# Linear attention on TensorE: keys x values by column halves, queries x state by row halves, queries laid out transposed

## Chip, cores and metric

One core of a Trainium2 chip runs the whole program. The metric is the device time of one execution in microseconds (us). The kernel before ran three times: 1289.58, 1290.80 and 1292.42 us, median 1290.8.

## What is computed

Three layers, one after another. Attention has no softmax, so keys and values collapse into one 64 x 64 state per batch and head:

```python
# batch, heads, seq, head_dim = 8, 8, 576, 64
kv  = np.einsum('bhsd,bhse->bhde', k, v)
out = np.einsum('bhsd,bhde->bhse', q, kv)
rms = np.sqrt(np.mean(out * out, axis=-1, keepdims=True) + 1e-06)
x   = out / rms * g_norm              # then tokens x 512: 4608 x 512
h   = x @ w_in                        # 512 x 2048, weights arrive as float64
x   = (h * np.cos(h)) @ w_out         # 2048 x 512
# routed layer: tokens with x @ w_skip > 0 go to the best of 8 experts
# (w_gate), y = gate * (relu(x @ w1[e]) @ w2[e]), added to x
```

## The kernel before, in words

The 4608 tokens are cut into 12 blocks of 384 tokens (`NB`, `TB`), each of three tiles of 128 tokens (`TPB`). A batch has 576 tokens, so two batches (a pair) fill nine tiles, and the fifth tile of a pair straddles both batches.

**The order of the work.** `dense()` (L772) walks through 192 steps, each a block and one of 16 chunks of 128 hidden units. A step issues twelve matmuls of 384 columns (`mm1`, L305), the elementwise chain of h cos(h) on ScalarE and VectorE (L312 to L327), and, three steps late (`LAG`), nine matmuls of 512 columns (`mm2`, L340). Their operands are float32r, each cut into a high part and a rest, hence three products per operand pair. `slot(i)` (L699) says what goes beside a step. Block 0 runs its first ten chunks, then block 1 all 16, then block 0 the other six; from block 2 on the order is plain. After the last block come the experts (L802 on).

**Attention beside it.** `attend(n, s)` (L552) is one of 16 parts of the attention of block n, issued one block ahead: parts 0, 4 and 8 turn a tile of queries (`attn1`: four transposes on TensorE into a PSUM tile `pt`, L198, and a ScalarE copy, L201, then an SP load of the queries two tiles on), parts 2, 6 and 10 multiply it with the state (`attn2`, L212, or L209 and L210 on a straddling tile, into the PSUM tile `po`), square (ScalarE, L214), sum (VectorE, L215) and take a reciprocal root in eleven small VectorE operations (`rsqrt`), parts 3, 7 and 11 scale it (`norm`, L232), parts 5, 9 and 13 transpose the result and cut it into parts (`attn3`, L244 to L247). Parts 1 and 14 of some blocks, or 1 and 5 of block 1, compute keys x values for half of a batch's heads (`do_kv`) and load the keys and values of a later one on SP's queue.

**Keys x values.** Of a batch's 576 tokens, 512 lie as four per partition on 128 partitions and 64 remain (`krem`, `vrem`, two batches stacked on 128 partitions). A head's product is four products of 128 rows (L171) and one of 64 (L172), all into the same 64 partitions of PSUM: the lower half of the array's columns for even heads, the upper for odd. A head is finished before the next begins:

```python
for i in range(NPAIR // 2):
    for o in range(2):
        h = 2 * i + o
        dst = po[o * DH:(o + 1) * DH, i]
        for c in range(CM):
            T.matmul(dst, kt[:, h, c], vt[:, h, c], start=(c == 0), stop=False)
        T.matmul(dst, r[0][rows, half * 4 + h], r[1][rows, half * 4 + h], start=False, stop=True)
```

Two VectorE copies (L175, L176) put the results of two heads on the diagonal of a 128 x 128 block of zeros, `kvbd`, so that one product of 128 rows serves two heads of queries: four products of 128 x 128 x 128 per tile.

**The start** (L487 to L541). SP issues the loads in the order of need: keys and values of batch 0, remainders, the queries of block 0, then weights in turn with further attention operands. The work goes: keys x values of half the heads, three VectorE copies of queries (L194) and their transposes, the other heads, then `attn2` of three tiles into `acc0` to `acc2`, and `rsqrt`, `norm`, `attn3`. `split_w` (L269) decodes a chunk of float64 weights, given as words, by one ScalarE operation, three of VectorE (L287 to L289), a ScalarE copy and one of GpSimd (L292); 32 chunks are decoded beside the first 26 steps.

PSUM's eight banks: two for `ph`, three for `acc`, two for `pt` (transposes of attention and experts), one for `po`.

Of the kernel before, what the change touches and what calls it, by code (L numbers as in the profile page):

```python
# [23 lines left out]
P = 128  # L24
B, H, S, DH = 8, 8, 576, 64
N = B * S
D = H * DH
# [33 lines left out]
def layers(tc, q, k, v, g_norm, w_in, w_out, w_skip, w_gate, w1, w2, out):  # L61
# [4 lines left out]
    # for each expert, in a region of its own, the tokens that are sent to it with their logits  # L66
    rows = nc.dram_tensor("gate_rows", [E + 1, D], F32, kind="Internal").ap()
# [18 lines left out]
    # ------------------------------------------------------------------ attention and dense layer  # L86
# [5 lines left out]
    ps_t = ctx.enter_context(tc.tile_pool(name="ps_t", bufs=2, space=PS))  # L92
# [20 lines left out]
    # a partition holds successive tokens of the first block  # L113
    G.iota(tok[:, 0:TPB], pattern=[[1, TPB]], base=0, channel_multiplier=TPB)
    G.iota(tok[:, TPB:], pattern=[[P, (NB - 1) * TPB]], base=TB, channel_multiplier=1)
# [4 lines left out]
    bp = patt.enter_context(tc.tile_pool(name="attn2", bufs=2, side="right"))  # L120
    kvbd = [ap.tile([P, NPAIR, P], F32, name=f"kvbd{i}") for i in range(2)]
    for t in kvbd:
        G.memset(t, 0.0)

    rem = {}
    qm = {}
    kvt = {}

    def load_rem(pair):
        rem[pair] = tuple(ap.tile([P, H, DH], F32, name=f"{name}rem") for name in "kv")  # L130
        for i in range(2):
            for r, src in zip(rem[pair], (k, v)):
                SP.dma_start(r[i * SR:(i + 1) * SR], src[2 * pair + i, :, SM:S, :].rearrange("h s d -> s h d"))

    def load_q(t):
        """Tile 4 of a pair of batches holds the last 64 rows of the first and the first 64 of the second."""
        if t == 0:
            # the first three, in longer runs
            r = xp.tile([P, H, TPB, DH], F32, name="xl")
            SP.dma_start(r, q[0, :, 0:TB, :].rearrange("h (p j) d -> p h j d", j=TPB))  # L140
            for j in range(TPB):
                qm[j] = r[:, :, j]
            return
        pair, i = divmod(t, 9)
        r = wp.tile([P, H, DH], F32, name="wo14") if t == 5 else bp.tile([P, H, DH], F32, name="q")
        r0 = i * P
        for j, (lo, hi) in enumerate(((0, S), (S, 2 * S))):
            s0, s1 = max(r0, lo), min(r0 + P, hi)
            if s0 < s1:
                SP.dma_start(r[s0 - r0:s1 - r0], q[2 * pair + j, :, s0 - lo:s1 - lo, :].rearrange("h s d -> s h d"))  # L150
        qm[t] = r

    def load_kv(b, half, pool=ap, names=("kmain", "vmain")):
        hs = slice(half * (H // 2), (half + 1) * (H // 2))
        kt = pool.tile([P, H // 2, CM, DH], F32, name=names[0])
        SP.dma_start(kt, k[b, hs, 0:SM, :].rearrange("h (p c) d -> p h c d", c=CM))
        vt = pool.tile([P, H // 2, CM, DH], F32, name=names[1])
        SP.dma_start(vt, v[b, hs, 0:SM, :].rearrange("h (p c) d -> p h c d", c=CM))
        kvt[b, half] = kt, vt

    def do_kv(b, half):
        kt, vt = kvt.pop((b, half))
        r = rem[b // 2]
        rows = slice((b % 2) * SR, (b % 2) * SR + SR)
        po = ps_o.tile([P, NPAIR // 2, DH], F32, name="po")
# [20 lines left out]
    def attn1(t, s=None):  # L186
        pt = ps_t.tile([P, NPAIR, P], F32, name="pt")
        qt = qm.pop(t)
        if t < TPB:
            if t < 2:  # L190
                c = ap.tile([P, H, DH], F32, name=("xn", "tT")[t])
            else:
                c = st.tile([P, H, DH], F32, name="wt", bufs=4)
            V.tensor_copy(c, qt)  # L194
            qt = c
        qt = qt.rearrange("p h d -> p (h d)")
        for hp in range(NPAIR):
            T.transpose(pt[:, hp], qt[:, hp * P:(hp + 1) * P], ident)  # L198
        if s is None:
            s = ap.tile([P, NPAIR, P], F32, name="tT")  # L200
        A.copy(s, pt)  # L201
        qT[t] = s

    def attn2(t, po, xn, ssq):
        i = t % 9
        s = qT.pop(t)
        for hp in range(NPAIR):
            if i == 4:
                T.matmul(po[0:SR, hp], s[:, hp, 0:SR], kvbd[0][:, hp], start=True, stop=True)  # L209
                T.matmul(po[SR:P, hp], s[:, hp, SR:P], kvbd[1][:, hp], start=True, stop=True)  # L210
            else:
                T.matmul(po[:, hp], s[:, hp], kvbd[0 if i < 4 else 1][:, hp], start=True, stop=True)  # L212
        pov = po.rearrange("p n (two e) -> p (n two) e", two=2)
        A.activation(xn, pov, AF.Square)  # L214
        V.tensor_reduce(out=ssq, in_=xn, op=ALU.add, axis=AX.X)  # L215
        normt[t] = xn, pov
# [13 lines left out]
    def norm(t, y):  # L230
        xn, pov = normt.pop(t)
        o = V.tensor_tensor(out=xn, in0=pov, in1=y.unsqueeze(2).to_broadcast([P, H, DH]), op=ALU.mult)  # L232
        xnt[t] = xn
        return o

    def attn3(t):
# [5 lines left out]
        pt = ps_t.tile([P, KD, P], F32, name="pt")  # L242
# [6 lines left out]
    def new_w(which, f):  # L249
        """The two parts of a chunk of the first or the second weights."""  # L250
        if which == "i":
            wi[f] = wp.tile([P, 2, KD, P], F32R, name=f"wi{f}")
            return wi[f][:, 0], wi[f][:, 1]
        wo[f] = wp.tile([P, 2, D], F32R, name=f"wo{f}")
        return wo[f][:, 0], wo[f][:, 1]


    # a chunk's words lie where its two parts will
    def load_w(which, f):
        if f >= NF:  # L260
            return
        if which == "i":
            t = words[which, f] = wp.tile([P, KD, 2 * P], I32, name=f"wi{f}")
            SP.dma_start(t, w_in[:, 2 * f * P:2 * (f + 1) * P].rearrange("(c p) w -> p c w", p=P))
        else:
            t = words[which, f] = wp.tile([P, 2 * D], I32, name=f"wo{f}")
            SP.dma_start(t, w_out[f * P:(f + 1) * P, :])
# [41 lines left out]
    def chain_head(ph):  # L309
        """h cos(h) of h in turns: the nearest whole number off, then cos as a sine."""  # L310
# [38 lines left out]
    def hold(b):  # L349
        """Lays the sums over the first half of a block's chunks aside."""  # L350
        for j in range(TPB):
            t = st.tile([P, D], F32, name=f"tT{j}")
            (V.tensor_copy if j == 1 else A.copy)(t, acc[b][j])
            SP.dma_start(held[j * P:(j + 1) * P, :], t)

    def evac(b):
# [5 lines left out]
        for j in range(TPB):  # L362
# [7 lines left out]
            SP.dma_start(out[0:TB].rearrange("(p j) d -> p j d", j=TPB)[:, j] if b == 0 else out[r0:r0 + P, :], t[:, j])  # L370
# [8 lines left out]

    def score_pe1(b, s, j):  # L380
        pt = ps_t.tile([P, KD, P], F32, name="pt")
# [10 lines left out]
    def route(b, j0, n):  # L392
        """Sends tokens of n tiles of a block to the lists of their experts."""
# [39 lines left out]
    # experts' weights come in pieces of two chunks of rows; an expert's parts take the places of one half of  # L433
    # the dense layer's chunks, in turn: a chunk of the first weights those of two chunks, four tiles each
# [34 lines left out]
    # start  # L469
# [29 lines left out]
    for i in range(2):  # L499
        SP.dma_start(g2[i * DH:(i + 1) * DH], g_norm.unsqueeze(1))  # L500
# [434 lines left out]
```

## Time and profile before

| | us |
|---|---|
| median of three runs (lowest, highest) | 1290.8 (1289.58, 1292.42) |
| profiled execution, span (the time that is given of it) | 1291.6 |
| TensorE matmuls busy | 1242.5 (96%) |
| TensorE weight loads busy (beside matmuls) | 1107.2 (86%) |
| VectorE busy | 870.2 (67%) |
| ScalarE busy | 641.0 (50%) |
| GpSimd busy | 194.2 (15%) |
| DMA, mean over the span | 81 GB/s |

Busy shares are averages over stages with different limits. A matmul's duration runs from its start to its modelled end; neighbours overlap, so what an instruction occupies of TensorE is read from the distance of starts. In rows of the trace, PE is TensorE's matmuls, PEld its weight loads, DVE VectorE, ACT ScalarE, POOL GpSimd; an arrow `<-` behind idle time names what ended it. `128*64` in a TensorE row is the part of the array used, rows by columns, `128x64` the moving operand.

### The profile page before, as it was taken

The numbers are of one execution on the slowest core, as the hardware profiler recorded it, in microseconds if no ns is written. First come the engines' busy times: TensorE is split into PE (matmuls) and PEld (weight loads), VectorE is DVE, ScalarE is ACT, GpSimd is POOL, SyncE is SP. The second block draws the span as 40 slices with busy tenths as digits, with TensorE's granted clock in tenths as the row PEclk, the third lists the DMA queues.
The fourth block names the chain that finished last, engine by engine and source line by source line (L and its number), as shares of the span: only waits on it lengthen the run. The fifth ranks groups of instructions, "written<-read, shape, count | busy, mean of one in ns | idle before, by whom it ended". The sixth has DMA issues, their size and how long they took to land. (4 is left out here: it accounts for less than half of the span.)

```text
span 1291.6 us, 18853 instructions
## 1 busy us (share of the span) xinstructions
PE 1242.5 (96%) x6864; PEld 1107.2 (86%) x6864; DVE 870.2 (67%) x2215; ACT 641.0 (50%) x1215; POOL 194.2 (15%) x187
## 2 busy tenths in 40 slices
PE   5798999999999999999999999999989999999997
PEld 4676898898989889889898989999868889998886
DVE  3988968885949568495774948677694576655421
ACT  2655764455545455555554545555556354444310
POOL 1533202101000000100001000010353312212100
PEclk9789999999999999999999999999999999999999
DMA  9923132203011120210203001010322356444300
GB/s 306 330 90 97 35 122 66 91 9 85 14 32 51 33 75 9 66 34 10 66 9 98 18 9 34 9 33 3 134 81 91 114 171 201 135 158 163 104 18 21
DMA packets 99698, 104.17 MB, mean 81 GB/s; under 512 B 50841, under 2 KB 77465, under 8 KB 99474
## 3 DMA queue, kind: packets, MB, share of 16 engines
q1 hardware_dynamic: 94610, 93.50, 23.6%
q0 software_dynamic: 4992, 9.43, 2.3%
q8 instruction: 55, 0.90, 0.3%
q14 instruction: 41, 0.34, 0.1%
HBM read 88.21 MB, written 18.03 MB: 82 GB/s over the span
## 5 line engine op out<-in xcount | busy, mean ns | idle before, releaser
L305 PE MATMUL ph<-xh,wi 128*128 128x384 f32 x1536 | 432.0, 342 | 20.1 <-DVE tb L320 17.8
L340 PE MATMUL acc<-wo,gh 128*128 128x512 f32 x1152 | 372.2, 403 | 1.3 <-ACT gh L326 1.3
L305 PEld LDWEIGHTS ph<-xh,wi 128*128 128x128 f32 x1536 | 285.0, 190 | 37.1 <-DVE tb L320 25.8
L305 PE MATMUL ph<-xl,wi 128*128 128x384 f32 x768 | 262.1, 341 | 0.0
L340 PEld LDWEIGHTS acc<-wo,gh 128*128 128x128 f32 x1152 | 207.7, 189 | 37.0 <-ACT gh L326 1.8
L340 PE MATMUL acc<-wo,gl 128*128 128x512 f32 x576 | 227.9, 396 | 0.1
L377 DVE SCALAR_TENSOR_TENSOR junk<-x,wgb 128x512 f32<-128x512 f32 x297 | 217.1, 731 | 2.3 <-ACT x L368 0.4
L326 ACT CAST gh<-tb 128x384 fp32r<-128x384 f32 x192 | 98.9, 515 | 152.4 <-DVE tb L320 78.0
L312 ACT ACTIVATE ta<-ph 128x384 f32<-128x384 f32 x192 | 94.2, 491 | 155.8 <-PE ph L305 155.5
L305 PEld LDWEIGHTS ph<-xl,wi 128*128 128x128 f32 x768 | 146.1, 190 | 7.8
L320 DVE SCALAR_TENSOR_TENSOR tb<-ph,tb 128x384 f32<-128x384 f32 x192 | 106.6, 555 | 66.9 <-ACT tb L319 66.3
L317 DVE SCALAR_TENSOR_TENSOR tb<-ta,ph 128x384 f32<-128x384 f32 x192 | 105.7, 550 | 63.9 <-ACT ta L312 63.6
L327 DVE TENSOR_TENSOR gl<-tb,gh 128x384 fp32r<-128x384 f32 x176 | 106.6, 606 | 55.8 <-ACT gh L326 54.3
L318 ACT ACTIVATE tb<-tb 128x384 f32<-128x384 f32 x192 | 100.7, 524 | 80.5 <-DVE tb L317 77.7
L340 PEld LDWEIGHTS acc<-wo,gl 128*128 128x128 f32 x576 | 108.4, 188 | 25.6 <-POOL gl L327 0.5
L632 PE MATMUL ph<-xh,wi 128*128 128x384 f32 (+1 forms) x512 | 129.7, 332 | 0.0
L424 POOL DMA_INDIRECT sent<-sent,posi x36 | 37.0, 1028 | 604.4 <-DVE posi L421 560.9
L668 PE MATMUL acc<-wo,hh 128*128 128x512 f32 x384 | 122.1, 398 | 0.0
L319 ACT ACTIVATE tb<-tb,halfpi 128x384 f32<-128x384 f32 x192 | 118.6, 618 | 5.6
L632 PEld LDWEIGHTS ph<-xh,wi 128*128 128x128 f32 x512 | 91.8, 188 | 0.3
L632 PE MATMUL ph<-xl,wi 128*128 128x384 f32 (+1 forms) x256 | 84.9, 332 | 0.0
L668 PEld LDWEIGHTS acc<-wo,hh 128*128 128x128 f32 x384 | 71.1, 188 | 15.2 <-ACT hh L658 0.3
(192 smaller groups left out, 1365.1 us busy)
## 6 DMA issues: line engine op xcount, KB each, us to landing
raw<-in_moe_w SPq DMA_DIRECT2D x64, 512.0 KB, 4.5
out<-x SPq DMA_DIRECT2D x33, 256.0 KB, 2.1
wi<-in_moe_w_in SPq DMA_DIRECT2D x16, 512.0 KB, 8.8
wo<-in_moe_w_out SPq DMA_DIRECT2D x16, 512.0 KB, 8.9
kmain<-in_k SPq DMA_DIRECT2D x15, 512.0 KB, 4.0
vmain<-in_v SPq DMA_DIRECT2D x15, 512.0 KB, 5.2
q<-in_q SPq DMA_DIRECT2D x28, 256.0 KB, 3.1
wgb<-gate_rows SPq DMA_DIRECT2D x1, 2304.0 KB, 8.5
```

The costliest lines, as they stand in the source:

```text
L305: T.matmul(ph, wi[f][:, w, c], x[:, c], start=(n == 0), stop=(n == 3 * KD - 1))
L312: after[0] = A.activation(ta, ph, AF.Copy, bias=MAGIC)
L317: V.scalar_tensor_tensor(out=tb, in0=ta, scalar=-MAGIC, in1=ph, op0=ALU.add, op1=ALU.subtract)
L318: A.activation(tb, tb, AF.Abs)
L319: ee["sin"] = A.activation(tb, tb, AF.Sin, bias=halfpi[:, 0:1], scale=-TWOPI)
L320: V.scalar_tensor_tensor(out=tb, in0=ph, scalar=TWOPI, in1=tb, op0=ALU.mult, op1=ALU.mult)
L326: A.copy(gh, tb)
L327: (G if key[0] == 0 else V).tensor_tensor(out=gl, in0=tb, in1=gh.bitcast(F32), op=ALU.subtract)
L340: T.matmul(acc[b][j], x[:, js], wo[f][:, w], start=(f == first and n == 0), stop=(f == last - 1 and n == 2))
L377: V.scalar_tensor_tensor(out=junk, in0=x2[b][:, j], scalar=1.0, in1=wgb[0][:, e], op0=ALU.mult, op1=ALU.mult, accum_out=score[b][:, j, e:e ...
L632: m = T.matmul(ph, wi[half * KF + 2 * c + f // KD][:, w, f % KD], x[:, c, 0:n], start=(i == 0), stop=(i == 3 * KD - 1))
L668: ee["down"] = T.matmul(py, ee[h][:, f, js], wo[half * KF + f][:, w], start=(n == 0), stop=(n == 3 * KF - 1))
```

## The change

Queries reach the device transposed, as twelve arrays of 128 x 4 x 384 (`qt`), one load per block, so `attn1` is gone. Keys, values, remainders and weights are laid out by the host so that a partition's part of a load is one run. In `do_kv` the products of the 64 remaining tokens come first, and the order of the others puts the two column halves in turn. The result is copied at once into `kvs`, 64 columns per pair of heads, without the zeros. `attn2` multiplies per head: 64 rows of the array each, even heads on the lower rows and odd heads on the upper, into two PSUM banks (or two tiles). `norm` and the squares take their operands in that order. PSUM: `pt` has one bank, `po` two; the experts' transposes take `pt` and `po` in turn. Routing's weights come ready laid out, without transposes on the device and the trip through memory. The first block's tokens lie in their plain order. One `rsqrt` serves the first three tiles.

```diff
-    ps_t = ctx.enter_context(tc.tile_pool(name="ps_t", bufs=2, space=PS))
+    ps_t = ctx.enter_context(tc.tile_pool(name="ps_t", bufs=1, space=PS))
...
+    kvs = [ap.tile([P, NPAIR, DH], F32, name=f"kvs{i}") for i in range(2)]
...
+    def load_q(n, pool=ap):
+        qT[n] = pool.tile([P, KD, TB], F32, name="qt")
+        SP.dma_start(qT[n], qt[n])
...
+    def do_kv(b, half, ps=ps_o, name="po"):
...
+        po = ps.tile([P, NPAIR // 2, DH], F32, name=name)
         for i in range(NPAIR // 2):
             for o in range(2):
-                h = 2 * i + o
-                dst = po[o * DH:(o + 1) * DH, i]
-                for c in range(CM):
-                    T.matmul(dst, kt[:, h, c], vt[:, h, c], start=(c == 0), stop=False)
-                T.matmul(dst, r[0][rows, half * 4 + h], r[1][rows, half * 4 + h], start=False, stop=True)
-        dst = kvbd[b % 2]
-        prs = slice(half * 2, half * 2 + 2)
-        V.tensor_copy(dst[0:DH, prs, 0:DH], po[0:DH])
-        V.tensor_copy(dst[DH:P, prs, DH:P], po[DH:P])
+                h = half * 4 + 2 * i + o
+                T.matmul(po[o * DH:(o + 1) * DH, i], r[0][rows, h], r[1][rows, h], start=(i == 0), stop=False, skip_group_check=True)
+        for i in range(NPAIR // 2):
+            for c in range(CM):
+                for o in range(2):
+                    h = 2 * i + o
+                    T.matmul(po[o * DH:(o + 1) * DH, i], kt[:, h, c], vt[:, h, c], start=False, stop=(c == CM - 1), skip_group_check=True)
+        V.tensor_copy(kvs[b % 2][:, half * 2:half * 2 + 2], po)
...
-    def attn1(t, s=None):
...
+    def attn2(t, segs, xn, ssq):
+        n, j = divmod(t, TPB)
+        i = t % 9
+        q = qT[n]
         for hp in range(NPAIR):
...
+            es = slice(hp * DH, (hp + 1) * DH)
+            for lo, hi, kv in ((0, P, kvs[0 if i < 4 else 1]),) if i != 4 else ((0, SR, kvs[0]), (SR, P, kvs[1])):
+                for o in range(2):
+                    ds = slice(o * DH, (o + 1) * DH)
+                    T.matmul(segs[o][lo:hi, es], q[ds, hp, j * P + lo:j * P + hi], kv[ds, hp], start=True, stop=True)
+        xo = xn.rearrange("p (n o) e -> p o n e", o=2)
...
+        for o0, po in segs[2]:
+            n = 1 if len(po.shape) == 3 else 2
+            x = xo[:, o0] if n == 1 else xo
+            A.activation(x, po, AF.Square)
...
+    def spare(i):
+        return ps_t.tile([P, KD, P], F32, name="pt") if i % 2 == 0 else ps_o.tile([P, KD, P], F32, name="po")
...
     load_kv(0, 0)
-    load_rem0(0)
-    load_q(0)
+    load_rem(0)
     load_kv(0, 1, st)
+    load_q(0, st)
     load_ws(1)
...
     do_kv(0, 0)
-    attn1(0, st.tile([P, NPAIR, P], F32, name="tT0"))
-    attn1(1, st.tile([P, NPAIR, P], F32, name="tT1"))
-    attn1(2, st.tile([P, NPAIR, P], F32, name="tT2"))
-    do_kv(0, 1)
+    do_kv(0, 1, ps_t, "pt")
...
+    attend0(0, banks(ps_o.tile([P, 2, SM], F32, name="po")))
+    attend0(1, banks(*(ps_a.tile([P, NPAIR * DH], F32, name=f"acc{j}") for j in range(2))))
+    attend0(2, banks(ps_a.tile([P, NPAIR * DH], F32, name="acc2"), ps_h.tile([P, NPAIR * DH], F32, name="ph")))
+    y = rsqrt(ssq)
...
-        if s in (0, 4, 8):
-            t = t0 + s // 4
-            attn1(t)
-            if 5 < t + 2 < NB * TPB:
-                load_q(t + 2)
+        if s == 11 and 1 < n + 1 < NB:
+            load_q(n + 1)
...
+    def main(a):
+        a = a[:, :, 0:SM].reshape(B, 2, H // 2, P, CM, DH)
+        return a.transpose(0, 1, 3, 2, 4, 5)
...
+        "qt": q.transpose(0, 2, 1, 3).reshape(NB, TB, KD, P).transpose(0, 3, 2, 1),
+        "km": main(k), "vm": main(v), "kr": left(k), "vr": left(v),
```

## Rows read from the trace of the kernel before

**Rows 1.** Busy time in stretches: us, each engine's busy us (instructions), clock, DMA share, GB/s.
```profile
0.00:10.00 10.00, 1.70 (x12) 1.46 (x13) 0.28 (x3) 1.49 (x2) 3.36 (x20) 1.00 0.85 204
10.00:15.00 5.00, 4.16 (x30) 3.39 (x29) 0.68 (x3) 0.00 (x0) 0.00 (x0) 1.00 1.10 342
36.00:122.00 86.00, 71.68 (x370) 60.61 (x371) 74.21 (x126) 47.28 (x90) 40.88 (x30) 0.88 0.59 173
150.00:920.00 770.00, 769.85 (x4386) 691.67 (x4385) 551.09 (x1593) 407.55 (x764) 48.74 (x52) 1.00 0.15 44
920.00:1292.00 372.00, 355.40 (x1849) 315.99 (x1848) 204.16 (x407) 153.83 (x302) 90.86 (x78) 1.00 0.35 115
```

**Rows 2.** Waits of TensorE from 150 to 920 us: us in total, times, longest.
```profile
PE ph L305 <- DVE tb L320: 0.2, 1, 0.2
```

**Rows 3.** TensorE in order of time, 452 to 495 us: start, us, what.
```profile
453.65 0.34 PE L305 MATMUL ph<-xh,wi 128*128 128x384 f32 x1
...
458.30 0.34 PE L305 MATMUL ph<-xh,wi 128*128 128x384 f32 x1
...
460.50 0.68 PE L171 MATMUL po<-vmain,kmain 128*64 128x64 f32 x8
461.11 0.32 PE L172 MATMUL po<-vrem,krem 64*64 64x64 f32 x2
461.37 0.68 PE L171 MATMUL po<-vmain,kmain 128*64 128x64 f32 x8
...
466.14 0.34 PE L305 MATMUL ph<-xh,wi 128*128 128x384 f32 x1
...
471.24 0.34 PE L305 MATMUL ph<-xh,wi 128*128 128x384 f32 x1
...
489.83 0.34 PE L305 MATMUL ph<-xh,wi 128*128 128x384 f32 x1
...
494.03 0.34 PE L305 MATMUL ph<-xh,wi 128*128 128x384 f32 x1
```

**Rows 4.** Groups by line and shape, 150 to 920 us: busy us, mean ns, idle before.
```profile
L171 PE MATMUL po<-vmain,kmain 128*64 128x64 f32 x384 | 32.6, 228 | 0.0
...
L212 PE MATMUL po<-kvbd,tT 128*128 128x128 f32 x216 | 28.4, 275 | 0.0
...
L201 ACT COPY tT<-pt 128x512 f32<-128x512 f32 x29 | 17.1, 588 | 0.0
...
L209 PE MATMUL po<-kvbd,tT 128*64 128x128 f32 x24 | 3.3, 279 | 0.0
```

**Rows 5.** Matmuls and weight loads of a straddling tile in order of time.
```profile
797.15 0.27 PE L209 MATMUL po<-kvbd,tT 128*64 128x128 f32 x1
797.15 0.14 PEld L209 LDWEIGHTS po<-kvbd,tT 128*64 128x64 f32 x1
797.15 0.27 PE L210 MATMUL po<-kvbd,tT 128*64 128x128 f32 x1
797.16 0.14 PEld L210 LDWEIGHTS po<-kvbd,tT 128*64 128x64 f32 x1
...
797.26 0.27 PE L209 MATMUL po<-kvbd,tT 128*64 128x128 f32 x1
```

**Rows 6.** TensorE in order of time around small products of nine columns.
```profile
1004.50 0.73 PE L389 MATMUL po<-wg,xh 128*128 128x9 f32 x6
1005.08 0.36 PE L632 MATMUL ph<-xh,wi 128*128 128x256 f32 x1
```

**Rows 7.** TensorE's start in order of time; last, VectorE at 88 us.
```profile
7.35 1.08 PE L171 MATMUL po<-vmain,kmain 128*64 128x64 f32 x8 [7.35 <-DMA vmain<-in_v]
...
24.19 2.00 PE L212 MATMUL acc<-kvbd,tT 128*128 128x128 f32 x16
...
36.00 1.20 PE L305 MATMUL ph<-xh,wi 128*128 128x384 f32 x2 [0.78 <-ACT xh L246]
...
88.22 0.28 DVE L175 COPY kvbd<-po 64x128 f32<-64x128 f32 x1 [3.15 <-PE po L172]
```

More of the change, by code (lines that the diff above doesn't have):

```diff
@@ L130, in load_rem @@
         rem[pair] = tuple(ap.tile([P, H, DH], F32, name=f"{name}rem") for name in "kv")
[L131 to L151, printed above, removed]
-    def load_kv(b, half, pool=ap, names=("kmain", "vmain")):
[L154 to L161, printed above, removed]
+        for r, src in zip(rem[pair], (kr, vr)):
+            SP.dma_start(r, src[pair])
+    def load_q(n, pool=ap):
+        qT[n] = pool.tile([P, KD, TB], F32, name="qt")
+        SP.dma_start(qT[n], qt[n])
+    def load_kv(b, half, pool=ap, names=("kmain", "vmain")):
+        t = [pool.tile([P, H // 2, CM, DH], F32, name=name) for name in names]
+        for x, src in zip(t, (km, vm)):
+            SP.dma_start(x, src[b, half])
+        kvt[b, half] = t
+    def do_kv(b, half, ps=ps_o, name="po"):
         kt, vt = kvt.pop((b, half))
@@ L204, in attn2 @@
[L204 to L214, printed above, removed]
-        V.tensor_reduce(out=ssq, in_=xn, op=ALU.add, axis=AX.X)
-        normt[t] = xn, pov
+    def attn2(t, segs, xn, ssq):
+        n, j = divmod(t, TPB)
+        i = t % 9
+        q = qT[n]
+        for hp in range(NPAIR):
+            es = slice(hp * DH, (hp + 1) * DH)
[4 more added lines that the diff above has]
+        xo = xn.rearrange("p (n o) e -> p o n e", o=2)
+        normt[t] = xn, []
+        for o0, po in segs[2]:
+            n = 1 if len(po.shape) == 3 else 2
+            x = xo[:, o0] if n == 1 else xo
+            A.activation(x, po, AF.Square)
+            normt[t][1].append((x, po, o0))
+        V.tensor_reduce(out=ssq, in_=xn, op=ALU.add, axis=AX.X)
@@ L218, in rsqrt, with banks @@
+    def banks(a, b=None):
+        if b is None:
+            v = a.rearrange("p o (n e) -> p o n e", e=DH)[:, :, 0:NPAIR]
+            return a[:, 0], a[:, 1], [(0, v)]
+        return a, b, [(o, x.rearrange("p (n e) -> p n e", e=DH)) for o, x in enumerate((a, b))]
     def rsqrt(ssq):
@@ L230, in norm, with attn3 @@
     def norm(t, y):
-        xn, pov = normt.pop(t)
-        o = V.tensor_tensor(out=xn, in0=pov, in1=y.unsqueeze(2).to_broadcast([P, H, DH]), op=ALU.mult)
+        xn, parts = normt.pop(t)
+        yo = y.rearrange("p (n o) -> p o n", o=2)
+        for x, po, o0 in parts:
+            r = yo[:, o0] if len(po.shape) == 3 else yo
+            o = V.tensor_tensor(out=x, in0=po, in1=r.unsqueeze(len(po.shape) - 1).to_broadcast(list(po.shape)), op=ALU.mult)
         xnt[t] = xn
         return o
-    def attn3(t):
+    def attn3(t, ps=ps_t, name="pt"):
         xn = xnt.pop(t).rearrange("p h e -> p (h e)")
@@ L241, in attn3 @@
         xh, xl = xhl[b]
-        pt = ps_t.tile([P, KD, P], F32, name="pt")
+        pt = ps.tile([P, KD, P], F32, name=name)
         for c in range(KD):
@@ L349, in hold @@
     def hold(b):
+        t = st.tile([P, TPB, D], F32, name="qt")
         for j in range(TPB):
-            t = st.tile([P, D], F32, name=f"tT{j}")
-            (V.tensor_copy if j == 1 else A.copy)(t, acc[b][j])
-            SP.dma_start(held[j * P:(j + 1) * P, :], t)
+            (V.tensor_copy if j == 1 else A.copy)(t[:, j], acc[b][j])
+            SP.dma_start(held[j * P:(j + 1) * P, :], t[:, j])
     def evac(b):
@@ L369, in evac @@
             r0 = (b * TPB + j) * P
-            SP.dma_start(out[0:TB].rearrange("(p j) d -> p j d", j=TPB)[:, j] if b == 0 else out[r0:r0 + P, :], t[:, j])
+            SP.dma_start(out[r0:r0 + P, :], t[:, j])
         score[b] = sp.tile([P, TPB, E + 1], F32, name="score")
@@ L653, in up_rows @@
         for g in range(2):
-            pt = ps_t.tile([P, KD, P], F32, name="pt")
+            pt = spare(g)
             for c in range(KD):
@@ L711, in slot @@
             if f == 7:
-                pt = ps_t.tile([E + 1, KD, P], F32, name="pt")
-                for c in range(KD):
-                    T.transpose(pt[:, c], wg[:, c], ident)
-                r = ap.tile([E + 1, KD, P], F32, name="tT")
-                A.copy(r, pt)
-                SP.dma_start(rows.rearrange("e (c p) -> e c p", c=KD), r)
                 fill_lst()
@@ L910, in layers, with laid_out, left @@
     ctx.close()
-_INS = ["q", "k", "v", "g_norm", "moe_w_in", "moe_w_out", "moe2_w_skip", "moe2_w_gate", "moe2_w1", "moe2_w2"]
+def laid_out(q, k, v, g_norm, moe_w_in, moe_w_out, moe2_w_skip, moe2_w_gate, moe2_w1, moe2_w2):
+    import numpy as np
+    def main(a):
+        a = a[:, :, 0:SM].reshape(B, 2, H // 2, P, CM, DH)
+        return a.transpose(0, 1, 3, 2, 4, 5)
+    def left(a):
+        a = a[:, :, SM:S].reshape(B // 2, 2, H, SR, DH)
+        return a.transpose(0, 1, 3, 2, 4).reshape(B // 2, P, H, DH)
+    rows = np.concatenate([moe2_w_gate.T, moe2_w_skip[None]])
+    return {
+        "qt": q.transpose(0, 2, 1, 3).reshape(NB, TB, KD, P).transpose(0, 3, 2, 1),
+        "km": main(k), "vm": main(v), "kr": left(k), "vr": left(v),
+        "g_norm": np.concatenate([g_norm, g_norm])[:, None],
+        "w_in": moe_w_in.reshape(KD, P, NF, P).transpose(2, 1, 0, 3),
+        "w_out": moe_w_out.reshape(NF, P, D),
+        "gates_p": rows.T.reshape(KD, P, E + 1).transpose(1, 0, 2), "gates_r": rows,
+        "w1": moe2_w1, "w2": moe2_w2,
+    }
 def kernel(**inputs):
```

86 lines of the change are left out of this document (23 added, 63 removed).

## The prediction

> **What bounds the kernel now.** I began with the busy time by stretches [rows 1]. From 150 to 920 us TensorE's matmuls cover 769.85 of 770 us at a granted clock of 1.00, the upper level (2.4 GHz), while VectorE has 551 and ScalarE 408. The list of what TensorE waited for in that stretch has one line, 0.2 us in all [rows 2]. So from 150 us on every instruction taken out of TensorE's stream shortens the run by what it occupies there. Before 122 us it is different: between 36 and 122 us TensorE has 71.7 us of 86, VectorE 74.2, and the clock averages 0.88. That stretch is set by decoding the weights on VectorE and by chains of waits.
>
> Next I took the price of each attention part from the order of time on TensorE [rows 3], as the distance between the first products of successive dense steps (durations of single matmuls overlap, distances do not). A bare step is 494.03 - 489.83 = 4.20 us. With four transposes of queries it is 458.30 - 453.65 = 4.65, so they cost 0.45. With half a batch's keys x values it is 466.14 - 458.30 = 7.84: 3.64. With one tile's queries x state it is 471.24 - 466.14 = 5.10: 0.90. How many of these fall in the saturated stretch is in the groups by line [rows 4]: 384/32 = 12 halves of keys x values, 216/8 = 27 ordinary query tiles (3 more straddle two batches), 29 query transposes by their ScalarE copies, with a thirtieth just ahead of it.
>
> **Part 1, the query transposes go.** 30 x 0.45 = 13.5 us off the bound engine. Their ScalarE copies, 17.1 us [rows 4], lie beside it and count nothing. The queries now come as one 768 KB load for three tiles, issued on SP behind the third tile's products and seven steps (about 30 us) ahead of use; at the 204 GB/s of the first 10 us [rows 1] it takes 4 us. I cost it at nothing; without that cover each of ten blocks would wait those 4 us.
>
> **Part 2, keys x values.** A float32 product is two passes in the trace: L171 has 32 per half [rows 4] where the program asks for 16. Within a head, eight passes of 64 columns take 461.11 - 460.50 = 0.61 us, 0.076 each, and the two passes with 64 rows 461.37 - 461.11 = 0.26 where two at 0.076 would be 0.15: 0.11 per head for changing tile shape to and fro [rows 3]. All ten passes of a head sit on one column half; the other idles. After, the eight 64-row passes come first, and all passes change column half at each product. The straddling tiles already do that: L209 and L210, on the two column halves, have matmuls that start together and weight loads 0.01 us apart, and the next pair follows after 797.26 - 797.15 = 0.11 us [rows 5]. Those stream 128 columns, mine 64, so a pair costs between 0.076 (a lone tile's pace) and 0.152 (no overlap). I take 0.08, near the lower end, because rows 5 show loads and matmuls side by side. Entering and leaving cost 3.64 - 4 x 0.87 = 0.16 now, one change of shape some 0.09 more: 0.25. New price: (4 + 16) pairs x 0.08 = 1.60, plus 0.25 = 1.85; 3.64 - 1.85 = 1.79, x 12 = 21.5 us. With the 0.11 of rows 5 a pair it is 1.19 each, 14 us; with no overlap 20 x 0.152 + 0.25 = 3.29, 4 us.
>
> The Trainium skill (TensorE: Matmul & The Clock Gate, The mechanism) says that a weight load overlaps running matmuls only when its row group differs; column halves share their rows, so by that rule this gain would be near 4 us. Rows 5 disagree with it for loads of the other column half. I follow the rows and keep the rule as a rival.
>
> VectorE's two copies per half (about 0.28 each) become one: 0.3 us off an engine that isn't the bound.
>
> **Part 3, queries x state.** Four products of 128 rows and 128 columns against a block-diagonal state become eight of 64 rows and 64 columns: 8 passes become 16, and each still loads 128 columns of weights (a tile's tokens). What a load costs when little streams past it is seen where nine columns stream: six passes take 1005.08 - 1004.50 = 0.58 us, 0.097 each [rows 6]. So loads alone are 16 x 0.097 = 1.55 us if the row halves take turns, 0.78 if they work side by side, against 0.90 now. No row of before has two row halves at work together. A pass of a full tile now takes 0.90/8 = 0.11 [rows 3]. The bounds: 0.78 with nothing added, gain 0.1 a tile; 16 x 0.11 + 0.2 for entering and leaving another shape = 2.0, loss 1.1. I take side by side, since rows 5 show it for column halves: 8 x 0.11 + 0.2 = 1.1, a loss of 0.2 x 27 = 5 us. The three straddling tiles go from 16 passes to 32 on quarters of the array: about nothing.
>
> The Trainium skill (same page, LDWEIGHTS) says that a load's time goes by its columns and not its rows, 128/1.2 = 107 ns here (an estimate from that page). Rows 6 agree (0.097), and the rule speaks against this part: halving the rows halves no load.
>
> The two-bank result tile is squared by ScalarE as one instruction, so VectorE's and ScalarE's work per tile stays. One transpose buffer less in PSUM: the experts' transposes alternate with the other tile, still two deep, and nothing else is close behind.
>
> **Part 4, the start.** Now the first product waits for data until 7.35 us, the last queries x state begin at 24.19 and the first dense product at 36.00 [rows 7]. The first 11.8 us step-by-step between those two (squares, sums, the chain of small VectorE operations, transposes) stays. What goes ahead of 24.19: three VectorE copies, twelve transposes, the second half's products in single file, the wait for VectorE in between. What is left is data: two halves of keys and values, the remainders of two batches and the queries, 3.4 MB. Bytes moved by 10 us are 204 x 10 = 2.0 MB, by 15 us 3.75 [rows 1], so 3.4 MB are there at about 14 us, larger runs helping a little. Half a batch's products at the lower clock are twice 1.6, so they end at about 14 too. Then 14.2 + 11.8 = 26: 10 us earlier, range 0 to 13. VectorE's decoding, continuous behind it, moves along, as weights are far ahead of use. Between 36 and 122 us I add 3 us: VectorE waits there for keys x values once for 3.15 us [rows 7], and those products get shorter. Bounds 0 and the 86 - 74 = 12 us in which VectorE idles.
>
> **Sum.** 13.5 + 21.5 - 5 + 10 + 3 = 43 us. The profiled execution spans 1291.6 us; its span lies between the runs shown (1289.58 to 1292.42), 0.8 above their median, so I use it as their time: 1291.6 - 43 = 1249. From 920 us on nothing changes but the tile that transposes use.
>
> **The rivals.** *Row halves take turns.* 2.0 us a tile instead of 1.1: 0.9 x 27 = 24 us back, 1273. For it: no row shows two row halves together, and rows 6 price sixteen loads in file at 1.55. Against: column halves do it. 0.20.
>
> *Column halves don't overlap at 64 columns.* A load of one half waits for the other half's matmul; part 2 gives 4 instead of 21.5 us: 1267. Against: rows 5, where four instructions on two halves begin within 0.01 us. 0.08. (This is what the Trainium skill's rule on row groups, named above, would give.)
>
> *The start doesn't move*, because VectorE's decoding (74 of 86 us) is bound by its own total and the weights by their loads: 10 us back, 1259. 0.07.
>
> *Slower: each change of row half empties the array.* Its place is queries x state, where the half changes at every product. A matmul there lasts 275 ns [rows 4] from start to end; if each of eight products must end before the other half starts, a tile takes 8 x (0.275 + 0.11) + 0.2 = 3.3 us, 2.2 more than forecast, x 27 = 59, and three straddling tiles with twice the changes add some 15: 1323. It turns the sign when a tile takes 1.1 + 43/27 = 2.7 us. For it: a shape change costs 0.11 in rows 3. Against: that is far below 275 ns, and changing column half costs nothing in rows 5. 0.05.
>
> **How the numbers follow.** The forecast as costed has 0.60, centre 1249. Its own bounds: part 2 up to 7 less or 1 more, part 3 8 better, part 4 from 13 less to 12 more; not all at one end, so 1232 to 1264. Taking in row halves in turn (1273) and the two smaller cases gives 1232 to 1276, leaving out the slow end of the rivals. Faster or slower counts from 0.2%, 2.6 us, about what the spread of runs lets one tell. All cases but the last are faster: 0.94 of chance, less a little for a mix of losses: faster 0.93, same 0.02, slower 0.05.
>
> **What would show it.** Right: no query transposes, bare steps at their places (4.20 us), steps with keys x values at 6.05 us with pairs of matmuls starting together, steps with queries x state at 5.3, first dense product near 26 us, the 770 us stretch shortened by about 30, TensorE still full. Wrong: queries x state steps at 6 us or more with matmuls in single file; keys x values steps above 7; gaps on TensorE waiting for VectorE after 150 us; a first dense product still near 36 us; a granted clock below 1.00 beyond 150 us.

## Result and profile after

The changed kernel takes 1244.08 us (median of 4 runs, 1243.34 to 1245.75) against 1291.61 for the kernel before beside it (4 runs): a ratio of 0.963, 95% interval 0.962 to 0.965. The forecast was 1249.0, range 1232 to 1276.

The profiled execution spans 1241.5 us. First its busy time in stretches, to be laid beside [rows 1]; the columns are the same (TensorE's matmuls, weight loads, VectorE, ScalarE, GpSimd, clock, DMA share, GB/s):

```profile
0.00:10.00 10.00, 2.25 (x38) 2.16 (x40) 0.28 (x3) 1.49 (x2) 2.34 (x17) 1.00 0.84 300
36.00:122.00 86.00, 71.70 (x423) 62.54 (x424) 77.49 (x139) 55.66 (x106) 41.19 (x31) 0.88 0.45 165
140.00:872.00 732.00, 730.80 (x4494) 651.08 (x4493) 540.08 (x1574) 386.64 (x726) 43.24 (x48) 1.00 0.13 46
872.00:1242.00 370.00, 353.51 (x1865) 316.92 (x1863) 204.17 (x409) 155.18 (x305) 94.49 (x81) 0.99 0.36 116
```

TensorE is still full in the long stretch (730.80 of 732) at a granted clock of 1.00, its upper level of 2.4 GHz. What it waited for there is three lines, 1.2 us in all (us in total, times, longest):

```profile
PE po L391 <- DVE xn L210: 0.6, 1, 0.6
PE acc L318 <- DVE x L344: 0.3, 1, 0.3
PE ph L283 <- DVE tb L298: 0.3, 1, 0.3
```

So, as before, a step is as long as its instructions occupy TensorE. TensorE in order of time shows a bare step, one with half a batch's keys x values (L149 the 64-row products, L154 those of 128 rows) and one with a tile's queries x state (L176); compare [rows 3]:

```profile
402.40 0.34 PE L283 MATMUL ph<-xh,wi 128*128 128x384 f32 x1
...
404.49 0.63 PE L318 MATMUL acc<-wo,gh 128*128 128x512 f32 x2
404.95 0.40 PE L318 MATMUL acc<-wo,gl 128*128 128x512 f32 x1
...
406.57 0.33 PE L283 MATMUL ph<-xh,wi 128*128 128x384 f32 x1
...
415.38 0.34 PE L283 MATMUL ph<-xh,wi 128*128 128x384 f32 x1
...
417.59 0.45 PE L149 MATMUL po<-vrem,krem 64*64 64x64 f32 x8
417.97 1.15 PE L154 MATMUL po<-vmain,kmain 128*64 128x64 f32 x32
419.05 0.73 PE L318 MATMUL acc<-wo,gh 128*128 128x512 f32 x2
419.62 0.39 PE L318 MATMUL acc<-wo,gl 128*128 128x512 f32 x1
...
421.23 0.33 PE L283 MATMUL ph<-xh,wi 128*128 128x384 f32 x1
...
435.68 0.33 PE L283 MATMUL ph<-xh,wi 128*128 128x384 f32 x1
...
437.88 1.11 PE L176 MATMUL po<-kvs,qt 64*128 64x64 f32 x16
438.92 0.74 PE L318 MATMUL acc<-wo,gh 128*128 128x512 f32 x2
...
441.12 0.34 PE L283 MATMUL ph<-xh,wi 128*128 128x384 f32 x1
```

Bare: 406.57 - 402.40 = 4.17 (4.20 before). Keys x values: 421.23 - 415.38 = 5.85, so 1.67 a half beside a step of 4.18, where it was 3.64. Queries x state: 441.12 - 435.68 = 5.44, so 1.26 a tile, where it was 0.90.

The start, in order of time on TensorE, beside [rows 7]; a bracket holds the wait that ended there:

```profile
7.75 0.69 PE L149 MATMUL po<-vrem,krem 64*64 64x64 f32 x8 [7.75 <-DMA vrem<-in_vr]
12.65 1.13 PE L176 MATMUL po<-kvs,qt 64*128 64x64 f32 x16
...
14.62 0.27 PE L176 MATMUL acc<-kvs,qt 64*128 64x64 f32 x1
14.62 0.27 PE L176 MATMUL ph<-kvs,qt 64*128 64x64 f32 x1
14.73 0.27 PE L176 MATMUL acc<-kvs,qt 64*128 64x64 f32 x1
14.73 0.27 PE L176 MATMUL ph<-kvs,qt 64*128 64x64 f32 x1
...
22.37 1.08 PE L222 MATMUL pt<-ident,kmain 128*128 128x128 f32 x4 [6.80 <-DVE kmain L210]
...
27.36 1.20 PE L283 MATMUL ph<-xh,wi 128*128 128x384 f32 x2 [0.92 <-ACT xh L224]
```

The first dense product comes at 27.36 us (36.00 before). The four rows from 14.62 on are the two row halves at work on a tile whose halves go to different PSUM tiles (`acc`, `ph`): a pair starts together, the next 0.11 us later.

**Where the 50 us between the two spans lie.** I use the starts of ScalarE's first operation of the dense steps, read from its order of time:

| | step 20 starts | steps 20 to 191 | step 191 to the end |
|---|---|---|---|
| before, us | 162.4 | 827.7 | 301.5 |
| changed, us | 147.5 | 796.9 | 297.0 |
| difference | 14.9 | 30.8 | 4.5 |

The last column was not expected: from there on the experts' products run, which nobody changed, and yet it is 4.5 us shorter.

### The profile page after: what moved, and what is told of

The parts are those of the page before. It is cut to its first block, busy times and chain, and to the rows that moved or that the text cites. A ratio compares the mean times of both kernels' runs of the same rounds, so it can differ in the third digit from the quotient of the medians.

```text
span 1241.5 us, 19058 instructions
## 1 busy us (share of the span) xinstructions
PE 1192.1 (96%) x7036; PEld 1062.4 (86%) x7036; DVE 858.1 (69%) x2187; ACT 621.4 (50%) x1180; POOL 191.6 (15%) x184
```

## Experiments

All times are medians; the kernel before stood at 1290.9 to 1291.7 beside each. Except where it says so, the edits are to the changed kernel.

**The changed kernel once more**, for its time and its pace.

> The changed kernel once more, unaltered, for comparison with the three beside it: 1244 us, 0.963 of the kernel before. Its profile also tells whether the pace of the dense layer's own matmuls differs from one execution to the next: in the two profiles at hand a bare dense step took 4.20 us before and 4.18 after, and an expert's 24 matmuls of 512 columns 5.63 before and 5.52 after, with no change to either. If that is the execution, it will differ here again; if it is the change, it will be 4.18 and 5.52.

1244.54 us (ratio 0.965, 0.963 to 0.966). A bare step again takes 4.19 us (medians of the bare steps from 165 to 930 us: 4.19 in both profiles of the changed kernel, 4.21 before): the pace of the unchanged products belongs to the kernel, not to one execution.

**Undo part 1 alone.** Four transposes per tile return to TensorE, of data that is transposed already and into a PSUM tile that nobody reads:

```diff
+        if s in (0, 4, 8):
+            pt = ps_t.tile([P, KD, P], F32, name="pt")
+            for c in range(KD):
+                T.transpose(pt[:, c], qT[n][:, c, s // 4 * P:(s // 4 + 1) * P], ident)
         if s in (2, 6, 10):
```

> The four transposes per query tile are put back on TensorE beside the unchanged rest, into a PSUM tile that nothing reads. Theory: they cost what they occupy, 30 x 0.45 = 13.5 us, and up to 2 in block 1: 1258 to 1260. Rival: without the ScalarE copy they fit into gaps, and the copy or the loads were what the old form cost: 1246 or less.

1259.59 us (0.975, 0.973 to 0.976): 15 more. Steps 20 to 191 take 810.1 us in place of 796.9, 13.2 more; the rest lies ahead of step 20.

**Only ScalarE's copies return** (the same place, `A.copy` of a tile of queries into an unused tile).

> The ScalarE copy per query tile is put back alone (from the loaded queries into a tile that nothing reads), 33 x 0.59 = 19 us of ScalarE. Theory: nothing, ScalarE is half idle: 1244, at most 2 more from the start. Rival: the copy delays the elementwise chain of its step, and TensorE with it: 1250 or more.

1244.18 us (0.963, 0.962 to 0.965): here 20.3 us of copies run on ScalarE and the time stays, so those of before (17.1 us in [rows 4]) had indeed been covered.

**Column halves in file**: the heads of a pair one after the other, the eight 64-row products still first.

```diff
-            for c in range(CM):
-                for o in range(2):
+            for o in range(2):
+                for c in range(CM):
```

> Keys x values keep everything but the turn of column halves: a head's eight passes of 128 rows follow each other on one half. Theory: the halves work side by side, which saves 4 x 0.61 - 1.08 = 1.36 us per half batch; undone, 12 x 1.36 = 16 us come back where TensorE is full and some 5 us at the start: 1265. Rival: the gain came from grouping the 64-row products, and the turn gives nothing: 1246.

1249.76 us (0.968, 0.967 to 0.969), 5 us more, not 20. In order of time:

```profile
419.97 1.54 PE L154 MATMUL po<-vmain,kmain 128*64 128x64 f32 x32
421.44 0.73 PE L318 MATMUL acc<-wo,gh 128*128 128x512 f32 x2
```

The 32 passes take 1.47 us, between the two expected prices. Heads that follow each other lie on different halves, and the starts in the trace show that a head does not wait for the one before to be through: the second head's first pass starts at 420.26 us, 0.01 behind the fifth of the first head's eight, and the other three run side by side with it. (The rows don't name the half; two trains of starts, each 0.058 us apart, tell them apart.) This run therefore doesn't say what one half alone costs. The next one does.

**All heads on one column half.** Order and grouping by shape as in the changed kernel, but every product writes PSUM partitions 0 to 63, and two VectorE copies carry the state on:

```diff
-                T.matmul(po[o * DH:(o + 1) * DH, i], r[0][rows, h], r[1][rows, h], ...
+            T.matmul(po[:, h], r[0][rows, half * 4 + h], r[1][rows, half * 4 + h], ...
...
-                    T.matmul(po[o * DH:(o + 1) * DH, i], kt[:, h, c], vt[:, h, c], ...
+                T.matmul(po[:, h], kt[:, h, c], vt[:, h, c], ...
```

> The changed kernel, but the products of keys and values of all heads run on the lower column half of the array, in file; the 64-row products still come first and together, so that the tile shape changes as seldom as in the changed kernel. Two VectorE copies in place of one carry the state to its two row halves. Theory (the column halves work side by side, and that is what halves the passes): the 40 passes of a half follow each other at 0.058 us, 2.3 us and some 0.35 for the two changes of shape, about 2.65 in place of 1.67; 12 x 0.98 = 11.8 us more than the changed kernel's 1244.3: 1256 us (1254 to 1260). Rival (the 64-row and 128-row products only had to be kept apart, and the two column halves share the array's time anyway): 1.7 us a half, 1244 to 1246.

1259.39 us (0.975, 0.973 to 0.976), 15 more. In order of time:

```profile
438.76 0.68 PE L147 MATMUL po<-vrem,krem 64*64 64x64 f32 x8
439.36 2.08 PE L150 MATMUL po<-vmain,kmain 128*64 128x64 f32 x32
441.37 0.73 PE L316 MATMUL acc<-wo,gh 128*128 128x512 f32 x2
```

2.01 us where the changed kernel has 1.08, 0.60 where it has 0.38: 1.15 a half, 13.8 for twelve (steps 20 to 191 are 13.5 us longer). So of the 1.97 saved per half, 1.15 is the two column halves side by side. The other 0.82 is what is left for the grouping by tile shape, which no run undid by itself.

**Row halves in file**: for each tile first the four products of the lower row half, then those of the upper.

```diff
-        for hp in range(NPAIR):
+        for oo, hp in ((oo, hp) for oo in range(2) for hp in range(NPAIR)):
...
-                for o in range(2):
+                for o in (oo,):
```

> Queries x state keep the row halves, but the four products on the lower rows come first and then the four on the upper, not in turn. Theory: the row halves do overlap in the changed kernel, and its pace of 0.13 us for two passes is that of one load of 128 columns on each half; in file 16 passes take about 2.1 us instead of 1.04, 27 x 1.04 = 28 us more, and 3 at the start: 1275. Rival: the row halves already take turns, and the order changes nothing: 1244.

1259.99 us (0.975, 0.973 to 0.976), 15 more. A tile's 16 passes:

```profile
409.71 1.60 PE L176 MATMUL po<-kvs,qt 64*128 64x64 f32 x16
411.24 0.72 PE L318 MATMUL acc<-wo,gh 128*128 128x512 f32 x2
```

1.53 in place of 1.04, not the 2.1 expected. That it is near the 1.55 which the prediction had for loads in file (16 x 0.097) is chance, for these passes are not all in file. The starts form two trains again, passes 0.111 us apart in each; the second begins at 410.21 us, 0.01 behind the fifth pass of the first, so three passes of each half run side by side. Steps 20 to 191 are 13.1 us longer; the rest lies ahead of step 20.

**Undo part 3**: the block-diagonal state and products of 128 x 128 return, with two copies of the state as before.

```diff
+                T.matmul(segs[lo:hi, hp], q[:, hp, j * P + lo:j * P + hi], kv[:, hp], start=True, stop=True)
```

> Queries x state go back to the full array, with the block-diagonal state and its two VectorE copies per half; transposed queries and column halves stay. Theory: this one part of the change loses, 0.36 us a tile; a step with it falls from 5.44 to 5.08 us, 27 x 0.36 = 10 us less: 1234. Rival: the second copy and the zeros are what the row halves save, so that the gain is lost on VectorE: 1244.

1241.73 us (0.962, 0.960 to 0.963), 2.6 less than the changed kernel, not some 10. A tile's eight passes take 0.81 us (a straddling tile's sixteen 1.02 where quarters take 0.62), and steps 20 to 191 are 5.9 us shorter, but step 20 starts 4.1 us later (151.6). So the steady steps lose by part 3, as forecast. The products alone would have given more: 27 tiles are 0.37 us a step shorter than in the changed kernel and three straddling ones 0.39 longer, some 8.8 in all. But twice from step 20 on TensorE waits just ahead of a tile's products, 1.6 and 0.9 us, which it doesn't do there in the changed kernel. Why the first twenty are slower here I did not follow up beyond their waits (until 155 us TensorE waits 12.8 us for the chain of h cos(h), 7.0 in the changed kernel).

**Quarters for every tile.** The other way to mend part 3: each product's tokens are cut in two as well, as the straddling tiles have it.

```diff
-            for lo, hi, kv in ((0, P, kvs[0 if i < 4 else 1]),) if i != 4 else ((0, SR, kvs[0]), (SR, P, kvs[1])):
+            for lo, hi, kv in ((0, SR, kvs[0 if i <= 4 else 1]), (SR, P, kvs[0 if i < 4 else 1])):
```

> Every query tile is multiplied as the straddling tiles are: by quarters of the array (64 rows, 64 columns), 32 passes instead of 16. Theory: what bounds queries x state now is that each pass loads 128 columns of weights, and loads on different halves run side by side; four quarters then take 0.63 us (as the straddling tiles do) instead of 1.04, the step 5.03 instead of 5.44 us, 27 x 0.41 = 11 us less in all: 1233. Rival: the number of passes bounds it, and twice as many take longer: a step of 6 us and 1260.

1235.71 us (0.957, 0.956 to 0.958), 8.6 less than the changed kernel, not 11:

```profile
436.70 0.69 PE L176 MATMUL po<-kvs,qt 64*64 64x64 f32 x32
437.32 0.74 PE L318 MATMUL acc<-wo,gh 128*128 128x512 f32 x2
```

Twice as many passes, 32, take 0.62 us where 16 took 1.04. Four quarters work together: four passes start within 0.02 us, and the next four 0.06 later; a pair of row halves takes 0.11. Each pass here loads 64 columns in place of 128. A step with a tile is 0.41 us shorter, as expected, 11 us for 27, but steps 20 to 191 only 8.3: at 222 us TensorE waits 1.9 us for VectorE's `x` (L344; 0.3 in the changed kernel), and behind that wait the granted clock falls to its lower level (1.2 GHz) for a while, 0.96 in the mean of 200 to 240 us where the changed kernel has 1.00.

**Loads as they were**: keys, values and remainders come from their old layout in 256-byte to 1 KB runs; the queries stay transposed.

> Keys, values and remainders are loaded from their plain layout, in runs of 1 KB and 256 bytes as before, four loads for a pair's remainders instead of two; all else stays. Theory: the first product, which needs 1.6 MB at 7.75 us, begins 1 to 3 us later, and the run ends as much later, 1245 to 1247. Rival A: VectorE's decoding hides it, 1244. Rival B: the larger runs are most of the 15 us that the first 20 steps gained, 1252 or more.

1247.41 us (0.966, 0.965 to 0.968): 3 us more, all at the start (step 0 starts at 35.2 us in place of 32.1; the later distances stay). Not all of it is shown to be the loads'. The queries x state begin at 14.50 us in place of 12.65, and 0.78 of that is a wait for values that the changed kernel doesn't have. The transposes behind them come at 25.56 in place of 22.37, another 1.3 lost, with these products running at a slower pace: a matmul lasts 0.42 us, 0.27 in the changed kernel. The run with the transposes returned and the padded one below have that slower pace too, with the loads unchanged. So 3 us is the most that the longer runs are worth.

**Where the operands lie.** In the changed kernel one call of `rsqrt` serves three tiles of tokens in place of two, so its two scratch tiles grew, and all that is allocated behind them lies 128 bytes further on each partition. First a pad that takes this back (modulo 1024 bytes):

```diff
     sp = ctx.enter_context(tc.tile_pool(name="small", bufs=2))
+    for _ in range(2):
+        G.memset(sp.tile([P, 112], F32, name="pad"), 0.0)
```

> The changed kernel with 896 unused bytes a partition in the pool of small tiles, filled once with zeros. This lays the gated values, the experts' hidden values and every later tile of the left side at the same offset, counted in 1024 bytes, as in the kernel before (the changed kernel has them 128 bytes further, because two small tiles grew). Theory (where the operands lie sets the pace of the matmuls that nobody changed): a step's first twelve products are back from 2.098 to 2.111 us, the experts' second products from 394 to 398 ns in the rows, and the whole is some 4 us longer, 1248 us (1247 to 1250). Rival (the pace hangs on something else, such as the banks of PSUM or the order of the instructions): both stay, 1244 us (1243 to 1246).

1254.32 us (0.970, 0.969 to 0.972): 10 more, where I had expected 4. The reverse, in the kernel **before**: scratch tiles of the changed kernel's size, no instruction added.

```diff
-        y, w = (sp.tile(list(ssq.shape), F32, name=n) for n in "yw")
+        m = math.prod(ssq.shape[1:]) // H
+        y, w = (sp.tile([P, TPB, H], F32, name=n)[:, 0:m] for n in "yw")
+        if len(ssq.shape) == 2:
+            y, w = y[:, 0], w[:, 0]
```

> The kernel before, with the two scratch tiles of the root's steps allocated for three tiles of tokens, as they are in the changed kernel, in place of two; the same columns of them are used, and no instruction is added or removed. Every tile behind them in the left side of SBUF lies 128 bytes further, at the offsets that the changed kernel has. Theory (these 128 bytes set the pace of the matmuls that nobody changed, as the padded run showed the other way round): the experts' second products take 394 ns in the rows in place of 398, twelve first products 2.098 us in place of 2.111, and the whole is 6 to 8 us shorter: 1284.5 us (1283 to 1287), so that some 7 of the change's 47 us are owed to this and not to its products. Rival (the padded run was longer by its start and by something else that the pad moved): 1290 to 1292 us, the rows as before.

1283.98 us against 1291.34 (0.9945, 0.9931 to 0.9958): 7.4 less, from addresses alone. The groups by line and shape from 950 us on show it (busy us, mean ns of one, idle before), the experts' first and second products; first the kernel before:

```profile
L668 PE MATMUL acc<-wo,hh 128*128 128x512 f32 x384 | 122.1, 398 | 0.0
L632 PE MATMUL ph<-xh,wi 128*128 128x384 f32 x448 | 116.2, 338 | 0.0
L668 PE MATMUL acc<-wo,hl 128*128 128x512 f32 x192 | 76.0, 396 | 0.0
L632 PE MATMUL ph<-xl,wi 128*128 128x384 f32 x224 | 75.7, 338 | 0.0
```

The kernel before with the larger scratch tiles:

```profile
L671 PE MATMUL acc<-wo,hh 128*128 128x512 f32 x384 | 120.4, 394 | 0.0
L635 PE MATMUL ph<-xh,wi 128*128 128x384 f32 x448 | 114.9, 334 | 0.0
L671 PE MATMUL acc<-wo,hl 128*128 128x512 f32 x192 | 75.2, 392 | 0.0
L635 PE MATMUL ph<-xl,wi 128*128 128x384 f32 x224 | 74.9, 334 | 0.0
```

The changed kernel, and the changed kernel with the pad:

```profile
L630 PE MATMUL acc<-wo,hh 128*128 128x512 f32 x384 | 120.3, 394 | 0.0
L594 PE MATMUL ph<-xh,wi 128*128 128x384 f32 x448 | 115.0, 334 | 0.0
```
```profile
L632 PE MATMUL acc<-wo,hh 128*128 128x512 f32 x384 | 122.1, 398 | 0.0
L596 PE MATMUL ph<-xh,wi 128*128 128x384 f32 x448 | 116.2, 338 | 0.0
```

The rows follow the offset and nothing else: 398 and 338 ns with the old one, 394 and 334 with the new, in either kernel. Busy time over the four groups is 390.0 against 385.4 us, 4.6 less, and the stretch from step 191 on is 301.5 against 297.0. In the dense steps a bare step takes 4.19 us (4.21 before; medians of the bare steps from 165 to 930 us), and steps 20 to 191 are 2.8 us shorter. 4.6 + 2.8 = 7.4. Expected there had been 2.098 us for twelve first products; they stay at 2.11 in both (medians of the bare steps), and it is the nine second ones that take 2.081 us in place of 2.095. So the gain of a dense step lies elsewhere in it than I had put it.

The padded run's other 3 us are at its start (step 0 at 34.3 us in place of 32.1). The first data come 0.7 us later (8.46, 7.75), and the products behind them run at the slower pace told above:

```profile
17.20 0.42 PE L178 MATMUL acc<-kvs,qt 64*128 64x64 f32 x1
...
17.41 0.42 PE L178 MATMUL acc<-kvs,qt 64*128 64x64 f32 x1
```

A pair takes 0.21 us here, 0.11 in the changed kernel (14.62 to 14.73), at a granted clock of 1.00 from 12 to 18 us in both. As the run with the transposes returned shows the same without a pad, I don't put this to the addresses; what decides between the two paces stays open.

**The best of it**: quarters, and the left-over 64 rows as a fifth chunk of 128 rows, so that keys x values has one tile shape:

```diff
+                    x, y = (kt[:, h, c], vt[:, h, c]) if c < CM else (krem[:, half * 4 + h], vz[b % 2][:, half * 4 + h])
+                    T.matmul(po[o * DH:(o + 1) * DH, i], x, y, start=(c == 0), stop=(c == CM))
```

`vz` are two tiles, zeroed once, each with the left-over values of one batch of a pair in its own 64 rows.

> The queries x state products by quarters of the array for every tile, as in the run by quarters (1235.7 us), and the products of the 64 rows that are left over without a change of tile shape: the keys of two batches lie stacked in 128 rows, and for each batch the values lie in a tile of their own whose other 64 rows are zeros, so that they are a fifth chunk of 128 rows behind the four others. Theory: 40 passes as 20 pairs at 0.0585 us are 1.2 us, and with the way into and out of the halves about 1.35 in place of 1.67 a half: 12 x 0.3 = 3.6 us less than the run by quarters, 1232 us (1230 to 1234). Rival (the change of shape into and out of the halves is what costs, and that stays): 8 more passes of 128 rows cost what 8 of 64 rows did, 1235 to 1237.

1231.03 us (0.953, 0.951 to 0.954), 13 less than the changed kernel:

```profile
413.66 0.69 PE L152 MATMUL po<-vmain,kmain 128*64 128x64 f32 x16
414.18 0.29 PE L152 MATMUL po<-vz,krem 128*64 128x64 f32 x4
414.30 0.64 PE L152 MATMUL po<-vmain,kmain 128*64 128x64 f32 x16
414.76 0.29 PE L152 MATMUL po<-vz,krem 128*64 128x64 f32 x4
414.98 0.73 PE L316 MATMUL acc<-wo,gh 128*128 128x512 f32 x2
```

40 passes take 1.32 us where 8 and 32 took 1.46. That is 0.14 a half, half of what I expected, some 1.7 us (steps 20 to 191 are 1.9 shorter than in the run by quarters). That the total still came out as expected is luck: it is 4.7 less than by quarters because step 20 also starts 2.6 us earlier (145.3). The first products no longer wait for the remainders, and TensorE begins at 6.24 us, not 7.88, but the first dense product comes no earlier for it (27.83, 27.16 by quarters). What differs behind it is the granted clock: from 36 to 122 us it is 0.92 in the mean, 0.88 by quarters. No run shows that this belongs to the edit.

## Why the prediction held, and where its terms were off

The view was right: TensorE full, so every pass taken out counts. The total came within 5 us because errors of either sign met, which is luck. By steps, against the changed kernel's 47.5 us:

- **Part 1**, forecast 13.5: the run with the transposes returned gives 13.2 in steps 20 to 191. Right, ScalarE's copies at nothing included.
- **Part 2**, forecast 12 x 1.79 = 21.5: 12 x 1.97 = 23.6. Right in mechanism, both sizes in "20 pairs x 0.08, plus 0.25" were off. A pair costs (1.32 - 1.08)/4 = 0.06 us, from the four more pairs of the best version: less than the 0.076 that I had called a lone tile's pace, which was itself an average that held a change of shape (in the run on one half a lone pass follows the other at 0.058). The changes of shape cost more: 0.12 on the way in (417.59 - 415.38 = 2.21 against 404.49 - 402.40 = 2.09), 0.38 - 4 x 0.06 = 0.14 from 64 to 128 rows, 1.08 - 16 x 0.06 = 0.12 at the end and 0.11 in the first dense products behind (419.62 - 419.05 against 404.95 - 404.49). 20 x 0.06 + 0.49 = 1.69, measured 1.67.
- **Part 3**, forecast a loss of 0.2 a tile, 5 us: 0.36, 27 x 0.36 = 9.7. The eight pairs at 0.11 held (14.62 to 14.73); the "0.2 for entering and leaving" is 1.26 - 8 x 0.11 = 0.38, by the same changes of shape as above. The straddling tiles, put at nothing, gain 0.4 each, 1.2 in all: their 32 quarter passes are the 0.62 of the run by quarters, where the old sixteen take 1.02.
- **Part 4**, forecast 10 + 3: the first dense product moved by 8.6, step 20 by 14.9. Of the latter, 3.0 are in doubt: the kernel before with the larger scratch tiles has step 20 at 159.4, and its medians don't hold that gain (the spans differ by 10.3, the medians by 7.4; from 36 to 122 us its granted clock is 0.91, 0.88 before). That leaves 12, a remainder: no run takes the new order of the start back by itself. The forecast's 14.2 us for the queries x state became 12.65, and its 11.8 from there to the first dense product became 14.7: VectorE, reached earlier, now does the first decoding (L265 to L267, 1.8 us) between the sums of squares, one operation of the reciprocal root (L198) takes 1.25 us at 18.24, and the transposes wait for `norm` until 22.37. "At the lower clock" was no reading of the clock: the granted clock is 1.00 in the first 15 us, before [rows 1] as in the changed kernel. It is the passes that are slower there: in the changed kernel 32 of them take 1.91 us (8.37 to 10.28), 1.08 in the steady step.
- **"From 920 us on nothing changes"** is the step that failed. 4.5 us went there and some 2.8 in the dense steps, through the addresses of operands, which neither the code of the products nor a row of before shows. With it the terms make 13.2 + 23.6 - 9.7 + 1.2 + 12 + 7.4 = 47.7, and 47.5 were measured.
- **The base**: in every run with a time of its own the span is some 1.8 us below it (1241.5 and 1243.34 for the changed kernel). I took the span of before as the execution's time; by the same distance it was some 1293.4.

The rivals. *Row halves take turns*: rows at 14.62 show a pair's two starts together, and the run in file costs 13.1 us in steps 20 to 191. *Column halves don't overlap at 64 columns*: one half alone takes 1.15 us more for the same passes. The Trainium skill (TensorE: Matmul & The Clock Gate, The mechanism) lets a weight load overlap only where its row group differs; the two column halves share their rows, so by that rule the run on one half would have cost nothing more, and the traces contradict it here. *Each change of row half empties the array*: no, but a change of tile shape does cost 0.1 to 0.2 us each way. The Trainium skill (TensorEngine Tiling (Array Packing), Key Properties) says that changing the mode, and not just the tile, drains TensorE; it gives no price, and the traces agree with it. *The start doesn't move* fell with 27.36. The chances of all cases but the slower one add up to 0.95, not 0.94; nothing hangs on it.

## What to carry to other kernels

Price small products by distances of starts, the passes and the changes of tile shape apart: here a pair of 64-column passes was 0.06 us and a visit to another shape some 0.35 to 0.5, so the shapes are to be grouped and the whole array given work on each visit (quarters took back all that row halves had lost: a step with a tile takes 5.03 us, 5.10 before, 5.44 with row halves). The product that filled the array's rows gained nothing by halving them: cutting rows left each load's 128 columns and doubled the passes. And where a trace shows unchanged instructions at another pace, compare the addresses of their operands before believing that the change did it: 7.4 of these 47.5 us would have been there for a larger scratch tile.

## What the runs showed that I had not expected

- 128 bytes in the placement of tiles moved the matmuls' pace by 1% (398 to 394 ns, 338 to 334 in the rows), both ways. Which operand, and which rule of addresses, was not tried.
- The order in the program does not bind the halves fully: 32 passes with eight of a column half in file took 1.47 us, where the same on one half took 2.01 and alternating 1.08; three of each eight ran beside the next head's, and the row halves in file did the same.
- In the first 20 us the same products ran at one of two paces, a pair of row halves in 0.11 or 0.21 us, from one profiled run to the next, at a granted clock of 1.00. Small differences at the start (the run with loads as they were, the padded run) can't be read without looking at it.
